# Three groups of 512 columns for branch A's projection, with branch B's values and gate moved into the keys' product

## The chip, the core and the metric

The kernel runs on one NeuronCore of one Trainium2 chip. The metric is the device time of one execution, in microseconds. The kernel before takes 1475.5 us (median of 3 runs, 1475.44 to 1475.64). The profile of an execution tells what each engine does: PE is the matrix engine (PEld are its weight loads), DVE the vector engine, ACT the scalar engine, POOL the general engine, SP the engine that only issues transfers.

## The reference

The input `x` has 2048 rows of 512. Two attentions over it are mixed by a gate.

```
g = sigmoid((x * gate_w).sum(-1))
# A: 32 heads of 16; each row attends to rows i, i-2, ..., i-14
q, k, v = x @ A_wqkv                      # 512 x 1536
a = softmax(q.k[i - 2w] * scale) . v[i - 2w]  @ A_wo
# B: 32 heads of 16 queries, all with the same keys and values
q = x @ B_wq ; k = x @ B_wk ; v = x @ B_wv    # k, v: 2048 x 16
b = softmax(q.k * scale) . v  @ B_wo          # over all 2048 rows
out = g * a + (1 - g) * b
```

## The kernel before

**Exactness.** Products of the projections run in a reduced format. So each operand is split in a high part and a low part (`split`, L82), and each product is made of three: high by high, high by low, low by high (`three`, L179). The depth of 512 is cut into four pieces `c`, so a projection of one bank is 12 steps. Each step is two matmuls, one on the upper and one on the lower 64 rows of the matrix engine; they run beside each other and write two halves of a pair of banks, which are added later.

**The start (0 to about 26 us).** `x` is loaded transposed in 16 blocks (`xraw`), and split into `xh` and `xl`. The keys' product (`keys`, L182) multiplies the unsplit `x` with a 128-column matrix made of the 512 x 16 key weights repeated: in each half of 64 columns there are the keys twice over interleaved, the keys once more, and once more again. The last 16 rows of each half are then overwritten by a constant in `post` (the scale in `mk[:, 0]` and the bias in `mk[:, 2]`): they are the rows through which a query's maximum is subtracted.

**The stream of lumps (about 26 to 268 us).** A list `lumps` holds 14 products for B's queries (`("q", m)`) and then 64 for branch A (`("a", gg, j)`): for each of four groups `gg` of 384 columns, 16 blocks `j` of 128 rows. In the first group 18 columns more ride along: 16 of B's values and 2 of the gate, which go to `vst` and `gate`. After each A lump, ACT copies the two half banks out (`a_post`, L251 and L252, and L254 and L255 for the values and the gate), POOL adds them (L261), and every second lump SP stores both to `ad` in device memory (L268). The weights of the next group are loaded by POOL's queue and split by ACT and POOL (`load_wa`, `split_wa`) while the current group runs, one piece every second lump. They lie in two buffers, each for a whole group.

**The maxima.** Branch B needs for each query the largest score before it can take exponentials. A unit is four heads by 512 queries; there are 32 units and 64 half fills for each, 2048 in all. A fill is a matmul into a spare bank and a reduction on DVE. `stream` (L732) puts fills between the lumps' steps, when the planner's own clock says that a bank is free: `clk["pe"]`, `clk["act"]` and `clk["dve"]` are moved on by fixed durations (`T_R` and so on, L46), and nothing is measured. Two forms exist: plain ones (`fill_pair` L352, `fill_one` L361), and after the first lumps of A a form through half sums and half differences (`fill_diff` L424, `fill_sum` L437): a pair of matmuls, two absolute values on ACT (L432), then two more matmuls, each with one DVE instruction (L442). One such round does four half fills.

**The attention of B (about 266 to 1461 us).** 512 steps `s`, 16 for each unit. A step has two exponentials of 128 x 1024 on ACT (L489), four pairs of half-array matmuls around them (`exp_pair` L482) and the weighted sum (`weighted` L494). Between them the planner puts fills of later units: one pair a step, and a single where `singles` (L890) finds that pairs alone will not be enough. Twelve of the 16 output blocks are made between units (`out_phase`), the last four in `spread`, which begins when the fills are all done and takes up to four products a step. If the fills of a unit are late, `pause` (L904) makes them with nothing beside. Branch A's own arithmetic is a list of pieces on POOL (`work`, L987), which starts when the first group is stored.

Of the kernel before, what the change touches and what calls it, by code (L numbers as in the profile page):

```python
# [33 lines left out]
GC = P // AC  # L34
GN = GC * AN
VN = DH + 2
# [6 lines left out]
LEAD, M2S, M1S, E1S, PER_ROW = 3.0, 0.5, 0.3, 0.2, 20  # L43

# [5 lines left out]
def gated_mix_kernel(ctx, tc, xt, wa, wk, wq, wo_a, wo_b, out):  # L50
# [53 lines left out]
    GO = [0, GN + VN, 2 * GN + VN, 3 * GN + VN]  # L104


    raw = []
    for pool, tag, n in ((wp, "aext", 5), (p1, "wah", 3), (p1, "wah", 3), (p1, "wal", 3), (p1, "wal", 2)):
        rest = pool.tile([P, n, 512], F32, name="xraw", tag=tag, bufs=2)
        raw += [rest[:, k, :] for k in range(n)]  # L110
# [17 lines left out]
    def load_wa(gg, c):  # L128
        n = GN + (0 if gg else VN)
        waraw[gg, c] = p1.tile([P, GN + VN], F32, name="waraw", bufs=2)  # L130
        nc.gpsimd.dma_start(waraw[gg, c][:, :n], wa[c * P:(c + 1) * P, GO[gg]:GO[gg] + n])

    def split_wa(gg, c):
        nonlocal pool
        n = GN + (0 if gg else VN)
        if c == 0:
            wah[gg] = p1.tile([P, C, GN + VN], F32R, name="wah", bufs=2)
            wal[gg] = p1.tile([P, C, GN + VN], F32R, name="wal", bufs=2)
        split(wah[gg][:, c, :n], wal[gg][:, c, :n], waraw.pop((gg, c))[:, :n], nc.gpsimd)
        pool = max(pool, clk["pe"] * 1e3) + 1100  # L140

    def ahead_wa(gg, k):
# [3 lines left out]
        if 2 < k <= 2 * C + 1 and k % 2:  # L146
            split_wa(gg, (k - 3) // 2)
# [34 lines left out]
    def keys(t):  # L182
# [49 lines left out]
    def a_project(gg, j):  # L232
        n = GN + (0 if gg else VN)
        t, r = j // 4, slice(j % 4 * P, (j % 4 + 1) * P)
        return three(lambda c: xh[t][c // 2][:, c % 2, r], lambda c: xl[:, t, c, r], lambda c: wah[gg][:, c, :n], lambda c: wal[gg][:, c, :n])

    def a_post(gg, j, x):

        nonlocal pool
        (bank, key), n = front[x], GN + (0 if gg else VN)  # L240
        settle("add", 1)
        if j % 2 == 0:
            settle("store", 1)
            stage["t"] = p1.tile([P, GC, 2, AN], F32, name="stage", bufs=2)
        st = stage["t"]
        if gg == 0 and j < 3:
            two = wp.tile([P, GN + VN], F32, name="two", tag="aext", bufs=2)
        else:
            two = (p2 if j % 3 else pm)[0].tile([P, GN + VN], F32, name="two", tag=("two", "raw", "own")[j % 3], bufs=1)
# [1024 lines left out]
```

## Time and profile before

| | |
|---|---|
| time, median of 3 runs | 1475.5 us |
| the profiled execution | 1475.43 us, of which the span of instructions is 1473.6 us |
| busy: PE, ACT, DVE, POOL | 99%, 86%, 81%, 70% of the span |
| A's lumps, first and last matmul | 76.0 us, 267.9 us |
| first and last start of an exponential (L489) | 266.5 us, 1460.1 us |

A busy share on PE is not a share of what it could do: its matmuls overlap, and their ends are modelled. So the prediction reads the distance from one start to the next. In a row of groups the numbers are: line, engine, operation, output and input, shapes, count, then busy time and mean duration in nanoseconds, then the idle time before and what ended it. In a row of waits they are the total, the number of times and the longest.

### The profile page before, as it was taken

Reading aid. Unit: us, or ns where it says so; the run is one execution under the profiler, and the core shown is the slowest. Engines: PE = TensorE matmul, PEld = TensorE weight load, DVE = VectorE, ACT = ScalarE, POOL = GpSimd, SP = SyncE. Lnnn points to the kernel's source line nnn. Section 1 sums busy time; section 2 is a strip of 40 time slices with the busy share of each in tenths; the row PEclk is TensorE's granted clock in tenths of the full one; section 3 lists DMA queues with packets and bytes.
Section 4 is the critical chain, followed back from the end, with each engine's and each line's share of the span. In section 5 each row is a group of like instructions: output and inputs, shape, how many; then the busy total and the mean of one; then the engine's idle time right before and its main releaser. Section 6 shows DMA issues by size and latency. Waiting matters only on the chain.

```text
span 1473.6 us, 29548 instructions
## 1 busy us (share of the span) xinstructions
PE 1461.7 (99%) x10996; PEld 708.0 (48%) x10996; DVE 1193.9 (81%) x1855; ACT 1274.5 (86%) x1646; POOL 1032.6 (70%) x1828
## 2 busy tenths in 40 slices
PE   9999999999999999999999999999999999999998
PEld 5999889533333333333333376333333364333333
DVE  6976667789888888888898878899888878889712
ACT  5468988899999999999999978999999988999986
POOL 7876988887888979888889898888888330111220
PEclk9999999999999999999999999999999999999999
DMA  6754323121220211202112121120120000000110
GB/s 224 209 151 136 93 88 120 34 85 42 66 80 7 85 60 42 71 12 71 45 38 77 36 64 67 42 71 26 57 71 12 12 27 16 13 1 2 29 31 30
DMA packets 54080, 89.86 MB, mean 61 GB/s; under 512 B 18800, under 2 KB 35232, under 8 KB 49712
## 3 DMA queue, kind: packets, MB, share of 16 engines
q1 hardware_dynamic: 46928, 48.99, 11.4%
q0 software_dynamic: 6432, 37.94, 7.8%
q8 instruction: 86, 1.41, 0.4%
q10 hardware_dynamic: 576, 1.05, 0.2%
q14 instruction: 58, 0.48, 0.1%
HBM read 60.07 MB, written 27.35 MB: 59 GB/s over the span
## 4 chain that ended last, share of the span: by engine, by line
PE 91%; ACT 3%; POOL 3%; issue 1%; DVE 1%; DMA 1%; DVEq 0%; POOLq 0%; ACTq 0%
PE po L497 35%; PE pe L487 23%; PE pm L330 8%; PE ps L330 7%; PE pe L1098 7%; PE pe L783 4%; PE pm L422 2%; PE ps L422 1%; PE pm L851 1%; ACT dd L432 1%; PE po L422 1%; POOL qlo L222 1%; POOL qraw L215 1%; PE pe L185 1%; DMA xraw<-xt 1%
## 5 line engine op out<-in xcount | busy, mean ns | idle before, releaser
L489 ACT ACTIVATE pexp<-pe 128x1024 f32<-128x1024 f32 x1022 | 989.5, 1022 | 93.0 <-PE pe L487 90.8
L357 DVE TENSOR_REDUCE mx<-pm 128x2 f32<-128x1024 f32 x495 | 605.8, 1224 | 117.6 <-PE pm L330 113.8
L497 PE MATMUL po<-pexp,vst 128*32 128x512 f32 x4096 | 545.7, 605 | 0.0
L487 PE MATMUL pe<-qst,kst 64*128 64x512 f32 x1916 | 434.5, 447 | 0.4 <-ACT pexp L489 0.3
L487 PEld LDWEIGHTS pe<-qst,kst 64*128 64x128 f32 x1916 | 179.7, 183 | 473.7 <-ACT pexp L489 467.8
L368 DVE TENSOR_REDUCE mx<-ps 128x1 f32<-128x512 f32 x481 | 327.1, 680 | 3.7 <-PE ps L330 3.7
L330 PE MATMUL pm<-kst,qst 62*128 62x512 f32 x945 | 192.0, 396 | 0.3 <-DVE mx L357 0.3
L561 POOL TENSOR_TENSOR pr<-aext 128x256 f32<-128x256 f32 x256 | 182.5, 738 | 2.2 <-DMA aext<-ad 1.9
L330 PE MATMUL ps<-kst,qst 62*128 62x512 f32 x455 | 180.0, 396 | 0.2 <-DVE mx L442 0.2
L621 POOL TENSOR_TENSOR oa<-oa,av 128x256 f32<-128x256 f32 x224 | 164.1, 732 | 15.1
L497 PEld LDWEIGHTS po<-pexp,vst 128*32 128x32 f32 x4096 | 80.8, 108 | 178.2 <-issue 169.1
L618 POOL TENSOR_TENSOR av<-aext,lg 128x256 f32<-128x256 f32 x224 | 139.3, 622 | 12.7
L1098 PE MATMUL pe<-wah,xh 64*128 64x384 f32 (+1 forms) x504 | 109.8, 338 | 0.4 <-ACT gate L255 0.4
L1098 PE MATMUL pe<-wal,xh 64*128 64x384 f32 (+1 forms) x504 | 110.1, 337 | 0.0
L1098 PE MATMUL pe<-wah,xl 64*128 64x384 f32 (+1 forms) x504 | 109.9, 337 | 0.0
L432 ACT ACTIVATE dd<-pm 128x512 f32<-128x512 f32 x164 | 91.0, 608 | 17.8 <-PE pm L422 11.3
L442 DVE CUSTOM_DVE_ANT_0 dd<-ps,dd 128x512 f32<-128x512 f32 x82 | 56.7, 692 | 55.1 <-PE ps L422 28.9
L330 PEld LDWEIGHTS pm<-kst,qst 62*128 62x128 f32 x945 | 92.0, 187 | 2.8 <-DVE mx L357 1.0
L330 PEld LDWEIGHTS ps<-kst,qst 62*128 62x128 f32 x455 | 85.0, 187 | 5.5 <-DVE mx L368 1.7
L567 POOL TENSOR_TENSOR tr<-pr 128x512 f32<-128x512 f32 x64 | 81.7, 1277 | 4.1
L567 POOL TENSOR_TENSOR tr<-tr 128x256 f32<-128x256 f32 (+1 forms) x128 | 72.4, 566 | 8.3
L524 POOL TENSOR_TENSOR rl<-rl,gate_t 128x16 f32<-128x16 f32 x31 | 6.8, 220 | 100.4 <-DVE rl L518 99.9
(215 smaller groups left out, 1896.2 us busy)
## 6 DMA issues: line engine op xcount, KB each, us to landing
aext<-ad POOLq DMA_DIRECT2D x32, 1056.0 KB, 5.5
ad<-stage SPq DMA_DIRECT2D x32, 384.0 KB
qst<-qd SPq DMA_DIRECT2D x60, 128.0 KB
xraw<-xt SPq DMA_DIRECT2D x16, 256.0 KB
qd<-qhi SPq DMA_DIRECT2D x16, 256.0 KB
qd<-qlo SPq DMA_DIRECT2D x16, 256.0 KB
qst<-qd SPq DMA_DIRECT2D x60, 64.0 KB
qst<-ml SPq DMA_DIRECT2D x216, 2.0 KB
```

Source lines behind the costliest of these rows:

```text
L330: nc.tensor.matmul(dst, qst[home(v)[0]][b:b + 62, pr, t * P:(t + 1) * P], kst[b:b + 62, kc * 512:(kc + 1) * 512], start=True, stop=True)
L357: nc.vector.tensor_reduce(m[:, :, pr, t, kc], dst, AX.X, ALU.max)
L368: nc.vector.tensor_reduce(m[:, odd, pr, t, kc:kc + 1], dst, AX.X, ALU.max)
L432: nc.scalar.activation(dd[0][:, odd], m2[:, odd, :], AF.Abs)
L487: nc.tensor.matmul(bank[:, odd, :], kst[b:b + 64, kt * P:(kt + 1) * P], qst[home(u)[0]][b:b + 64, pr, :], start=True, stop=True)
L489: nc.scalar.activation(e, bank, AF.Exp, scale=SCALE)
L497: nc.tensor.matmul(po[32 * i:32 * i + 32, :], vst[:, kt, :], pexp[s, i // 2][:, i % 2, :], start=(kt == 0), stop=(kt == NJ - 1))
L561: nc.gpsimd.tensor_mul(pr[:, k], q, e[:, o:o + NH, AC:2 * AC])
L567: nc.gpsimd.tensor_add(nx, cur[:, :, 0:n], cur[:, :, n:2 * n])
L618: nc.gpsimd.tensor_mul(av, e[:, o:o + NH, 2 * AC:].rearrange("p j (h d) -> p j h d", d=DH), lg[:, w].unsqueeze(3).to_broadcast([P, NH, AG, ...
L621: nc.gpsimd.tensor_add(ao, ao, av)
L1098: nc.tensor.matmul(front[2 if x == last else x % 2][0][:, b, :n], l[h], r[h], start=(i == 0), stop=(i == 3 * C - 1))
```

## The change

Branch A's 1536 columns are laid out group by head pair (`wa` is now in the order of `ad`), and are projected in 3 groups of 512 columns: 48 lumps instead of 64, each matmul 512 columns wide. A group boundary now falls inside a head pair, so a store of two lumps is made of pieces (`a_pieces`): whole head pairs, one transfer for each of the two lumps, and one or two part pairs. The values and the gate leave the first group; their weights take the last 16 columns of each half of the keys' matrix, which were overwritten anyway. A DVE transpose of each keys' bank is kept (`turned_k`), and 16 tasks of two small ACT copies bring them to `vst` and `gate`. The gate's exponential comes after query product 12 rather than at the end of the first group. The split weights lie in six single buffers for each part instead of two whole groups: pieces 2 and 3 of the next group are split during the last lump of the current one. Some of the planner's durations change.

```diff
-GC = P // AC
-GN = GC * AN
-VN = DH + 2
+GG = 3
+GN = NAG * AN // GG
+WB = 6
...
     def load_wa(gg, c):
-        n = GN + (0 if gg else VN)
-        waraw[gg, c] = p1.tile([P, GN + VN], F32, name="waraw", bufs=2)
-        nc.gpsimd.dma_start(waraw[gg, c][:, :n], wa[c * P:(c + 1) * P, GO[gg]:GO[gg] + n])
+        waraw[gg, c] = p1.tile([P, GN], F32, name="waraw", bufs=2)
+        nc.gpsimd.dma_start(waraw[gg, c], wa[c * P:(c + 1) * P, gg * GN:(gg + 1) * GN])
     def split_wa(gg, c):
...
-        if c == 0:
-            wah[gg] = p1.tile([P, C, GN + VN], F32R, name="wah", bufs=2)
-            wal[gg] = p1.tile([P, C, GN + VN], F32R, name="wal", bufs=2)
-        split(wah[gg][:, c, :n], wal[gg][:, c, :n], waraw.pop((gg, c))[:, :n], nc.gpsimd)
-        pool = max(pool, clk["pe"] * 1e3) + 1100
+        wah[gg, c] = p1.tile([P, GN], F32R, name="wah", bufs=WB)
+        wal[gg, c] = p1.tile([P, GN], F32R, name="wal", bufs=WB)
+        split(wah[gg, c], wal[gg, c], waraw.pop((gg, c)), nc.gpsimd)
+        after("act", clk["pe"], 0.62)
+        pool = max(pool, clk["pe"] * 1e3) + 1300
...
-        if 2 < k <= 2 * C + 1 and k % 2:
+        if 2 < k <= (2 * C if gg == 0 else 2 * (WB - C)) + 1 and k % 2:
             split_wa(gg, (k - 3) // 2)
...
             nc.vector.scalar_tensor_tensor(ks, pk, mk[:, 1:2], ks.bitcast(F32), op0=ALU.mult, op1=ALU.add)
+            nc.vector.transpose(turned_k[:, t, :], pk)
+    def values_of(t, q):
+        v = turned_k[32:64, t].rearrange("p (j b z) -> p j b z", b=4, z=32)[:, :, q, DH:2 * DH]
+        nc.scalar.activation(vst[32 * q:32 * q + 32, 4 * t:4 * t + 4, 0:DH], v, AF.Copy)
+        g = turned_k[96:128, t].rearrange("p (j b z) -> p j b z", b=4, z=32)[:, :, q, DH]
+        nc.scalar.activation(gate[32 * q:32 * q + 32, 1, 4 * t:4 * t + 4], g, AF.Copy)
+        after("act", clk["pe"], 0.45)
...
+    def a_store(st, gg, j, col, w, g, many, n):
+        src = st[:, :, col:col + w].rearrange("p j (g n) -> p g j n", g=many)
+        dst = ad[g:g + many, HALO:, :].rearrange("g (p j) n -> p g j n", j=NJ)[:, :, j - 1:j + 1, n:n + w // many]
+        if many > 1:
+            for x in range(2):
+                nc.sync.dma_start(dst[:, :, x], src[:, :, x])
+        else:
+            nc.sync.dma_start(dst[:, 0], src[:, 0])
...
-        nc.scalar.activation(own, bank[:, 0, :GN].rearrange("p (g n) -> p g n", g=GC), AF.Copy)
-        nc.scalar.activation(two[:, :n], bank[:, 1, :n], AF.Copy)
-        if gg == 0:
-            nc.scalar.activation(vst[:, j, 0:DH], bank[:, 0, GN:GN + DH], AF.Copy)
-            nc.scalar.activation(gate[:, 1, j:j + 1], bank[:, 0, GN + DH:GN + DH + 1], AF.Copy)
-        at = after("act", clk["pe"] + T_LAT, 0.8 if gg else 1.2)
+        nc.scalar.activation(own, bank[:, 0, :], AF.Copy)
+        nc.scalar.activation(two, bank[:, 1, :], AF.Copy)
+        at = after("act", clk["pe"] + T_LAT, 1.05)
...
-            nc.gpsimd.tensor_add(own, own, two[:, :GN].rearrange("p (g n) -> p g n", g=GC))
-            if gg == 0:
-                nc.gpsimd.tensor_add(vst[:, j, 0:DH], vst[:, j, 0:DH], two[:, GN:GN + DH])
-                nc.gpsimd.tensor_add(gate[:, 1, j:j + 1], gate[:, 1, j:j + 1], two[:, GN + DH:GN + DH + 1])
-            pool = max(pool, 1e3 * at) + (1000 if gg else 1450)
+            nc.gpsimd.tensor_add(own, own, two)
+            pool = max(pool, 1e3 * at) + 1280
+            def store():
+                for piece in a_pieces(gg):
+                    a_store(st, gg, j, *piece)
...
+    for k in range(16):
+        tasks.append((31.0 + 1.5 * k, values_of, divmod(k, 4)))
...
-                yield lambda: order[i][0] // GC < ready_gg
+                yield lambda: (AN * (order[i][0] + 1) - 1) // GN < ready_gg
...
-        return T_R if n == 512 else 0.18
+        return T_R
...
+        if lump[0] == "a" and lump[2] == NJ - 1 and lump[1] + 1 < GG and i in (4, 7) and WB - C < 4:
+            c = WB - C + (i == 7)
+            if c < C:
+                split_wa(lump[1] + 1, c)
...
+            if m == 12:
+                gates()
...
     def whole(gg):
         nonlocal ready_gg
-        if gg == 0:
-            gates()
         ready_gg += 1
...
+    wide = np.repeat(bk, 2, axis=1)
-        "wk": np.tile(np.concatenate([np.repeat(bk, 2, axis=1), bk, bk], axis=1), (1, 2)).reshape(C, P, P).transpose(1, 0, 2),
+        "wk": np.concatenate([wide, bk, bv, wide, bk, np.repeat(gw, DH, axis=1)], axis=1).reshape(C, P, P).transpose(1, 0, 2),
```

More of the change, by code (lines that the diff above doesn't have):

```diff
@@ L103, in gated_mix_kernel @@
     waraw, wah, wal = {}, {}, {}
[L104 to L110, printed above, removed]
+    first = wp.tile([P, 4, 512], F32, name="xraw", tag="aext", bufs=2)
+    raw = [first[:, k, :] for k in range(4)]
+    raw += [p1.tile([P, 512], F32, name="xraw", tag=tag, bufs=WB) for tag in ("wah", "wal") for _ in range(6)]
     xraw = {(t, c): raw[C * t + c] for t in range(NQB) for c in range(C)}
@@ L1074, in gated_mix_kernel @@
     lumps += [("q", m) for m in range(2, 4 * NQB)]
-    lumps += [("a", gg, j) for gg in range(C) for j in range(NJ)]
+    lumps += [("a", gg, j) for gg in range(GG) for j in range(NJ)]
     ready_gg, items = 0, {}
```

38 lines of the change are left out of this document (23 added, 15 removed).

## The prediction, made before the result was known

> **What bounds the kernel now.** I read the page first, then the stretches, then the order of time inside each stretch that the change touches.
>
> ```profile
> span 1473.6 us, 29548 instructions
> PE 1461.7 (99%) x10996; PEld 708.0 (48%) x10996; DVE 1193.9 (81%) x1855; ACT 1274.5 (86%) x1646; POOL 1032.6 (70%) x1828
> PE 91%; ACT 3%; POOL 3%; issue 1%; DVE 1%; DMA 1%; DVEq 0%; POOLq 0%; ACTq 0%
> ```
>
> The chain of work that ended last is PE's to 91%. So what counts is PE's work and the few places where PE waits. The stretches (times from the span's start; busy us of PE, PEld, DVE, ACT, POOL, with the number of instructions; then clock, DMA share, GB/s):
>
> ```profile
> 0.00:26.00 26.00, 24.45 (x72) 14.19 (x72) 14.21 (x27) 13.16 (x23) 18.99 (x25) 1.00 0.79 264
> 26.00:76.00 50.00, 49.23 (x416) 44.13 (x417) 48.05 (x61) 25.13 (x38) 45.19 (x39) 1.00 0.69 192
> 101.00:268.00 167.00, 165.87 (x1673) 151.77 (x1672) 111.54 (x345) 144.15 (x336) 137.71 (x223) 1.00 0.35 109
> 268.00:1392.00 1124.00, 1121.62 (x8053) 443.53 (x8051) 985.82 (x1361) 1017.53 (x1149) 795.10 (x1480) 1.00 0.14 44
> 1392.00:1473.00 81.00, 75.97 (x560) 32.11 (x558) 14.42 (x33) 61.84 (x66) 17.87 (x32) 0.99 0.12 30
> ```
>
> B's queries (26 to 76) have DVE and POOL full beside PE. In A's lumps with the half-sum fills (101 to 268) ACT is busy 144.15 of 167 us, the nearest to PE. From 268 to 1392 everything waits for steps of exponentials with fills between them; after 1392 there are no fills, only the last output blocks. The profiled execution took 1475.43 us, 1.8 us of them outside the span, 0.1 us under the median of 1475.5. My sum is made against 1475.4.
>
> **The lumps' matmuls.** Three excerpts of the order of time, for 512, 402 and 384 columns; the first and last start of an even run:
>
> ```profile
> 57.18 0.41 PE L1098 MATMUL pe<-xh,wqh 64*128 64x512 f32 x2
> 58.34 0.41 PE L1098 MATMUL pe<-xl,wqh 64*128 64x512 f32 x2
> ...
> 100.75 0.42 PE L1098 MATMUL pe<-wal,xh 64*128 64x402 f32 x2
> 101.86 0.41 PE L1098 MATMUL pe<-wal,xh 64*128 64x402 f32 x2
> ...
> 164.27 0.34 PE L1098 MATMUL pe<-wah,xl 64*128 64x384 f32 x2
> 164.98 0.34 PE L1098 MATMUL pe<-wah,xh 64*128 64x384 f32 x2
> ```
>
> They are 5, 6 and 4 steps apart, so a step takes 0.232, 0.185 and 0.1775 us. Before: 16 x 12 x 0.185 + 48 x 12 x 0.1775 = 35.5 + 102.2 = 137.7 us. After: 48 x 12 x 0.232 = 133.6 us. **Term 1: -4.1 us.** It is small because a step's time goes nearly with its columns: (0.232 - 0.1775) / 128 is 0.43 ns a column, which leaves 0.01 us a step that is saved by having fewer of them; the other half of the gain is the 18 columns of values and gate. The keys' product carries them free: its columns were computed before too.
>
> The Trainium skill, "TensorE: Matmul & The Clock Gate", section Back-to-back issue gap, gives columns / 2.4 + 2.5 ns for a warm matmul and so speaks against wide steps even more. By it the sum is 126.2 before and 124.3 after, a term of -1.9 and a total 2.2 us higher. Every step above is longer than this, 0.232 against 0.216 for 512, so I keep the rows.
>
> **What moves from ACT, POOL and DVE.** Groups of the lumps' stretches and of the start, and one line of the waits:
>
> ```profile
> L432 ACT ACTIVATE dd<-pm 128x512 f32<-128x512 f32 x164 | 91.0, 608 | 17.8 <-PE pm L422 11.3 <-DVE mx L442 5.9
> L252 ACT ACTIVATE two<-pe 128x384 f32<-128x384 f32 (+1 forms) x56 | 27.9, 499 | 0.0
> L251 ACT ACTIVATE stage<-pe 128x384 f32<-128x384 f32 x56 | 27.5, 492 | 5.2 <-PE pe L1098 3.0 <-POOL wal L84 0.8 <-PE po L422 0.4
> L442 DVE CUSTOM_DVE_ANT_0 dd<-ps,dd 128x512 f32<-128x512 f32 x82 | 56.7, 692 | 55.1 <-PE ps L422 28.9 <-ACT dd L432 23.2 <-ACT stage L251 1.4
> PEld pm L422 <- ACT dd L432: 11.3, 39, 0.7
> L83 ACT ACTIVATE wah<-waraw 128x384 fp32r<-128x384 f32 x11 | 5.9, 538 | 0.1
> L84 POOL TENSOR_TENSOR wal<-waraw,wah 128x402 fp32r<-128x402 f32 x4 | 3.9, 981 | 0.0
> L222 POOL TENSOR_TENSOR qlo<-qraw,qhi 128x512 fp32r<-128x512 f32 x14 | 18.1, 1290 | 5.4 <-ACT qhi L221 5.4
> L511 DVE STREAM_TRANSPOSE tt<-po 128x512 f32<-128x512 f32 x31 | 22.1, 714 | 1.1 <-PE po L497 0.5
> L287 ACT ACTIVATE gate_t<-gate 32x16 f32<-32x16 f32 x16 | 3.6, 228 | 0.4
> ```
>
> A copy of 512 columns is taken at the 608 ns of L432 (same shape). ACT's copies out: 64 x (499 + 492) = 63.4 us before, 48 x 2 x 608 = 58.4 us after.
>
> **Fewer maxima fit among the lumps.** The planner starts a round of four half fills when its own clocks say that ACT's absolute values are done. I walked these clocks by hand (L424 to L444 and L734 to L769). Undisturbed, a round lets 6 steps of 0.18 pass, or 5 steps of 0.23; a round into which a copy-out falls lets 8 or 7 pass. A lump of 12 steps is then 8 and two thirds of 6 before: 1.67 rounds, and 7 and 5 after: 2.0 rounds. Measured were 82 rounds (L442) in 56 lumps (L251), 1.46, which is 0.88 of the walk, as other ACT work disturbs it. After: 0.88 x 2.0 = 1.75 in the 40 lumps that are left after the same eight first ones: 70 rounds. So 12 rounds or 48 half fills fewer, less about 5 that the longer first eight lumps take in addition. A round is four matmuls in pairs, 2 x 0.232 us of PE. **Term 2: -5.6 us here**, paid back in term 6. Bounds: none lost (2.05 a lump) to 20 (1.55 a lump, if ACT's clock, now charged for the splits too, disturbs more rounds).
>
> **PE's waits among the lumps.** PE waited 11.3 us for the absolute values (the wait row). They come where ACT takes longer than planned: a copy-out is planned at 0.80 and takes 0.99 less overlap, a split of `wah` is not planned and takes 0.54. After, the copy-out is planned at 1.05 against 1.2 less overlap, and the split at 0.62. **Term 3: -4 us**; bounds 0 and -11.3. I take the lower third, since the two absolute values stay under-planned.
>
> **The queries' stretch gets slower.** The chain there, in order of time:
>
> ```profile
> 28.53 1.19 DVE mx L368 x2
> ...
> 60.25 0.89 POOL wal L84
> 61.14 1.26 POOL qlo L222
> ...
> 82.72 0.46 PE pe L1098 x2
> ```
>
> POOL's pieces run one behind the other. Four splits of the first group grow from 981 to 1290 ns: +1.2 us, which PE pays at 82.72, where the first of A's lumps waits for ACT behind the last query's parts. Four transposes of 714 ns come to DVE; three fall into the start, where it is busy 14.21 of 26 us, the fourth stands before the fills at 28.53: +0.7 us. The 32 small copies (228 ns each, 7.3 us in all) fit: ACT is busy 25.13 of 50 us there. If its gaps were not where they fall, two copies, 0.4 us, could delay each of eight queries, 3 us. **Term 4: +1.9 us**, bounds 0 and +5.
>
> **The weights at the two group boundaries.** Pieces 2 and 3 are split after steps 4 and 7 of the last lump and needed at steps 6 and 9 of the next, 14 steps later: with 1.75 rounds in a lump, (12 x 0.232 + 1.75 x 0.464) / 12 = 0.30 us a step, 4.2 us. In that time ACT must do 0.61 after what is queued, and POOL 1.29 each after its queue, which the planner lets run up to 2.5 us ahead plus one piece: 2.5 + 0.7 + 2 x 1.29 = 5.8, less the 0.9 us between the two. At the first boundary branch A's arithmetic has not begun, and POOL is free. Behind the waiting matmul PE's whole queue stands. **Term 5: +1.5 us**, at the second boundary; bounds 0 and +6.
>
> **Stores.** One transfer of 512 packets becomes three or four with 1536 in all.
>
> ```profile
> DMA  2000000000000499990000000000004999600000
> L268 SPq DMA_DIRECT2D ad<-stage x32: 359/366/396, 85.4 to 270.5; - x32
> 1152.44 0.73 POOL L621 TENSOR_TENSOR oa<-oa,av 128x256 f32<-128x256 f32 x1
> L672 PE MATMUL pe<-ident,oa x32: 213/222/274, 1187.0 to 1211.2; 64*128 64x64 f32 x32
> ```
>
> The first line cuts 160 to 172 us in 40; there are two stores in it. One holds the DMA engines for four slices of 0.3 us, 1.2 us. Three times the packets at the same time each would be 3.6 us, out of 7.3 us for two lumps (24 steps of 0.30). SP issues 4 x 0.37 us rather than 0.37, with nothing urgent behind it but queries' maxima for units far ahead. The buffer is used again three lumps after its last copy, 10.9 us, less the copies and POOL's add (1.2 + 1.29): 8.4 us. Cost 0; without that cover see the rivals. Branch A's arithmetic starts when the first group is stored, 16 x 12 x (0.232 - 0.185) = 9 us later; it ended at 1153 and its last results are first used at 1187, so that is hidden too.
>
> **The end.** What was not filled early must be filled late:
>
> ```profile
> 1372.16 1.07 PE L497 MATMUL po<-pexp,vst 128*32 128x512 f32 x8
> 1380.75 1.07 PE L497 MATMUL po<-pexp,vst 128*32 128x512 f32 x8
> 1382.64 1.07 PE L497 MATMUL po<-pexp,vst 128*32 128x512 f32 x8
> 1390.70 1.07 PE L497 MATMUL po<-pexp,vst 128*32 128x512 f32 x8
> 1392.03 0.88 PE L851 MATMUL pm<-woh,turned 64*128 64x512 f32 x6
> 1422.19 0.63 PE L851 MATMUL pm<-wol,own 64*128 64x512 f32 x4
> 1424.30 0.39 PE L851 MATMUL pm<-wol,own 64*128 64x512 f32 x2
> L357 DVE TENSOR_REDUCE mx<-pm 128x2 f32<-128x1024 f32 x468 | 572.9, 1224 | 111.8 <-PE pm L330 108.1 <-PE ps L330 0.2
> ```
>
> Four steps with a pair and a single take 8.59 us, 2.15 each; four with the pair alone 8.06, 2.02. Singles ran almost to the end: about five steps at 1382 to 1391 had room for one. So of 43 more half fills 5 are cheap (0.13 us each), and 38 need 13 further steps of three. The last blocks, which began at 1392.03 and ran three products in 2.11 us steps, then have 20 steps instead of 33 for their 84 products (ten may follow): four a step, 20 x 0.232 = +4.6 us. The fills of the last unit are also due by step 488, some four steps too early; the rest goes in a pause at 1.22 us a pair (L357) with little beside, +2.4 us. **Term 6: +7 us**; bounds 0 (no rounds lost) and +23 (19 pairs all in pauses).
>
> **Sum.** -4.1 - 5.6 - 4 + 1.9 + 1.5 + 7 = -3.3, so 1472.1 us, called **1472 us**. About 3 us, 0.2%, is what a measurement here can tell from no change.
>
> **The rivals.**
> *The fills keep up* (22%). If the rounds stay at 82, nothing is moved, terms 2 and 6 go, and shorter lumps are kept whole: -4.1 - 4 + 1.9, without the stall: 1469; with the longer waits gone too, 1464. For it: two full rounds a lump in the walk. Against it: 0.88 of them ran.
> *The end overflows* (24%). If 60 half fills or more are missing, the last unit's maxima are not ready, and each further pair is a pause of 1.22 us: 10 pairs more, +12 us, about 1483. It decides from some 50 missing half fills on. For it: DVE is busy 986 of the 1124 us from 268 to 1392 already. Against it: the output blocks' own rounds lie between.
> *The weights come late* (10%). Both boundaries at the full bound: +6 rather than +1.5, with the queries at +5: 1479.
> *The stores hold the staging buffers* (4%). If a short packet takes twice as long, a store takes 8 us and more, and every third lump waits about 1 us, some 20 us: 1490. The low load (0.35 of the engines) speaks against it.
>
> **Chances.** The forecast itself has 40%, with its own range of 1468 to 1476, half of it under 1472.5. Faster by over 0.2%: half of 40 and the 22, 42%. Within: the other half and a part of the late weights, 25%. Slower: 33%. The range over the cases is 1463 to 1484.
>
> **What would show it.** 48 lumps at 0.232 us a step; A's last lump ending some 8 us earlier, at 260; 70 rounds (L442 with `dd` 140) instead of 82; the queries' stretch ending 2 us later; the last blocks' products starting nearer to the last exponential. Wrong would be: as many rounds as before, PE waiting for `wal` or `wah` by microseconds, waits of ACT for `stage` stores, or pauses before step 496.

## The result and the profile after

The kernel after takes 1477.97 us (median of 20 runs, 1477.59 to 1480.71), the kernel before beside it 1475.42 us (20 runs, 1475.21 to 1476.48). The ratio is 1.0019 with a 95% interval of 1.0012 to 1.0026: the change makes the kernel slower by about 0.2%. The prediction said 1472 and faster.

The page of the profile after, its span, its engines and the chain of work that ended last:

```profile
span 1475.9 us, 28719 instructions
...
PE 1462.1 (99%) x10612; PEld 681.4 (46%) x10612; DVE 1210.2 (82%) x1851; ACT 1269.2 (86%) x1592; POOL 1023.9 (69%) x1772
...
PE 87%; DVE 1%; ACT 1%; SPq 1%; issue 0%; DMA 0%; DVEq 0%; ACTq 0%; POOL 0%
```

PE does less (10612 matmuls instead of 10996), but holds only 87% of the chain instead of 91%, and SP's queue has appeared in it with 1%. The stretches, columns as in the prediction:

```profile
101.00:268.00 167.00, 165.98 (x1360) 129.59 (x1360) 111.15 (x318) 139.40 (x272) 130.78 (x184) 1.00 0.40 108
268.00:1392.00 1124.00, 1122.58 (x8065) 444.06 (x8057) 987.55 (x1365) 1016.56 (x1146) 798.78 (x1485) 1.00 0.14 43
1392.00:1475.00 83.00, 75.13 (x529) 33.20 (x521) 26.86 (x44) 53.87 (x57) 15.54 (x28) 0.96 0.10 27
```

In the last one DVE is busy for 26.86 us instead of 14.42: there are fills now. And the clock, 0.99 before, is 0.96 on the mean. Where the time goes is seen best from the start of a step's first weighted matmul (L497 before, L518 after; 8 a step, read from the order of time):

| | before | after | difference |
|---|---|---|---|
| step 0 starts at | 269.1 | 260.6 | -8.5 |
| step 0 to 480 | 1124.0 | 1122.4 | -1.6 |
| 480 to 484 | 9.4 | 8.5 | -0.9 |
| 484 to 488 | 9.6 | 14.2 | +4.6 |
| 488 to 492 | 8.7 | 11.6 | +2.9 |
| 492 to 496 | 8.7 | 11.4 | +2.7 |
| 496 to 511 | 31.6 | 35.3 | +3.7 |
| 511 to the end of the span | 12.4 | 11.8 | -0.6 |

At step 480 the kernel after is 10.1 us ahead. In the last 32 steps it loses 12.4. The lead is that of one trace: seven kernels below are edits that have the same lumps, and their traces reach step 480 8.5 to 10.4 us ahead, but for `a_kt0`, which spends more time before it. The order of time of PE at the end:

```profile
1397.12 0.40 PE L351 MATMUL pm<-kst,qst 62*128 62x512 f32 x2
1397.35 0.40 PE L508 MATMUL pe<-qst,kst 64*128 64x512 f32 x2
1397.60 0.39 PE L351 MATMUL ps<-kst,qst 62*128 62x512 f32 x1
1397.91 1.06 PE L518 MATMUL po<-pexp,vst 128*32 128x512 f32 x8
1398.91 0.51 PE L351 MATMUL pe<-kst,qst 62*128 62x512 f32 x2
1399.24 0.40 PE L351 MATMUL pm<-kst,qst 62*128 62x512 f32 x2
1399.48 0.40 PE L351 MATMUL pe<-kst,qst 62*128 62x512 f32 x2
1400.80 0.51 PE L351 MATMUL pe<-kst,qst 62*128 62x512 f32 x2 [0.93 <-DVE mx L378]
1401.93 0.50 PE L351 MATMUL pm<-kst,qst 62*128 62x512 f32 x2 [0.62 <-DVE mx L378]
1404.19 1.22 PE L508 MATMUL pe<-qst,kst 64*128 64x512 f32 x4 [1.76 <-DVE mx L378]
1405.21 0.62 PE L351 MATMUL ps<-kst,qst 62*128 62x512 f32 x1
1405.77 1.93 PE L518 MATMUL po<-pexp,vst 128*32 128x512 f32 x8
...
1410.98 1.10 PE L872 MATMUL pm<-woh,turned 64*128 64x512 f32 x8
...
1413.58 1.09 PE L872 MATMUL pm<-wol,turned 64*128 64x512 f32 x8
...
1424.46 0.69 PE L508 MATMUL pe<-qst,kst 64*128 64x512 f32 x2 [0.59 <-DMA qst<-ml]
```

Until 1398.9 the steps still have a pair and a single (L351). Then a pause: five pairs with nothing beside, the last two, and the step behind them, held up by DVE's reductions (L378). The first step behind it is odd: its eight weighted matmuls take 1.93 us, where the same eight took 1.06 at 1397.91. The stretches from the pause on say why; the clock is the third number from the end:

```profile
1398.91:1404.19 5.28, 1.97 (x14) 0.85 (x10) 5.14 (x6) 0.41 (x1) 0.00 (x0) 0.92 0.01 2
1404.19:1410.64 6.45, 6.45 (x27) 2.05 (x27) 3.46 (x7) 3.88 (x4) 0.34 (x2) 0.54 0.00 0
1410.64:1424.46 13.82, 13.24 (x106) 6.28 (x103) 1.90 (x5) 10.24 (x10) 6.33 (x12) 1.00 0.20 41
```

PE is busy for 1.97 of the 5.28 us of the pause. Before the pause ends its clock is halved, and it stays so nearly to the end of the next two steps. These two steps have 13 matmuls each (four for the exponentials, one fill, eight weighted) and take 6.45 us together; the same 26 take 4.00 us at full clock in `a_busy`, below. So the low clock costs 2.45 us. Behind that the products of the last blocks (L872) come four a step, 2.59 us from one step to the next. In the kernel before they come three a step, 2.36 us, and later two, 2.12 us. So the 12.4 us are, about: 5.3 us of pause and 2.45 of low clock (together the 7.5 between steps 484 and 492, within 0.3), then 6.4 us of crowded steps, the 0.59 us wait at 1424.46 among them, less the 1.5 us in the first and last row.

### The profile page after: what moved, and what is told of

The parts are those of the page before. It is cut to its first block, busy times and chain, and to the rows that moved or that the text cites. A ratio compares the mean times of both kernels' runs of the same rounds, so it can differ in the third digit from the quotient of the medians.

```text
span 1475.9 us, 28719 instructions
## 1 busy us (share of the span) xinstructions
PE 1462.1 (99%) x10612; PEld 681.4 (46%) x10612; DVE 1210.2 (82%) x1851; ACT 1269.2 (86%) x1592; POOL 1023.9 (69%) x1772
## 3 DMA queue, kind: packets, MB, share of 16 engines
q1 hardware_dynamic: 68176, 49.00, 11.7%
q10 hardware_dynamic: 576, 1.05, 0.2%
## 4 chain that ended last, share of the span: by engine, by line
PE 87%; DVE 1%; ACT 1%; SPq 1%; issue 0%; DMA 0%; DVEq 0%; ACTq 0%; POOL 0%
PE po L518 34%; PE pe L508 23%; PE pm L351 8%; PE ps L351 7%; PE pe L1124 5%; PE pe L804 4%; PE pm L443 2%; PE ps L443 1%; PE po L443 1%; PE pm L872 1%; SPq L728 0%; DVE mx L378 0%; PE pe L693 0%; ACT pexp L453 0%; DMA td<-raw 0%
## 5 line engine op out<-in xcount | busy, mean ns | idle before, releaser
L378 DVE TENSOR_REDUCE mx<-pm 128x2 f32<-128x1024 f32 x500 | 611.8, 1224 | 117.7 <-PE pm L351 114.8
L518 PE MATMUL po<-pexp,vst 128*32 128x512 f32 x4096 | 546.8, 606 | 0.1
L389 DVE TENSOR_REDUCE mx<-ps 128x1 f32<-128x512 f32 x494 | 336.1, 680 | 4.5 <-PE ps L351 4.5
L351 PE MATMUL pm<-kst,qst 62*128 62x512 f32 x942 | 192.2, 396 | 0.9 <-DVE mx L378 0.9
L351 PE MATMUL ps<-kst,qst 62*128 62x512 f32 x459 | 181.9, 396 | 0.4 <-DVE mx L463 0.2
L518 PEld LDWEIGHTS po<-pexp,vst 128*32 128x32 f32 x4096 | 80.6, 108 | 180.1 <-issue 171.6
L453 ACT ACTIVATE dd<-pm 128x512 f32<-128x512 f32 x150 | 85.0, 609 | 24.3 <-PE pm L443 21.2
L1124 PE MATMUL pe<-wal,xh 64*128 64x512 f32 x376 | 94.4, 392 | 0.2 <-POOL wal L84 0.2
L1124 PE MATMUL pe<-wah,xh 64*128 64x512 f32 x376 | 93.8, 392 | 0.1
L351 PEld LDWEIGHTS pm<-kst,qst 62*128 62x128 f32 x942 | 92.0, 187 | 3.7 <-DVE mx L378 1.6
L1124 PE MATMUL pe<-wah,xl 64*128 64x512 f32 x376 | 92.9, 392 | 0.0
L463 DVE CUSTOM_DVE_ANT_0 dd<-ps,dd 128x512 f32<-128x512 f32 x75 | 51.9, 692 | 48.3 <-PE ps L443 39.9
L351 PEld LDWEIGHTS ps<-kst,qst 62*128 62x128 f32 x459 | 85.8, 187 | 6.6 <-DVE mx L389 2.4
L281 POOL TENSOR_TENSOR stage<-stage,two 128x512 f32<-128x512 f32 x48 | 62.5, 1302 | 23.1 <-ACT two L275 22.6
```

The costliest lines, as they stand in the source:

```text
L351: nc.tensor.matmul(dst, qst[home(v)[0]][b:b + 62, pr, t * P:(t + 1) * P], kst[b:b + 62, kc * 512:(kc + 1) * 512], start=True, stop=True)
L378: nc.vector.tensor_reduce(m[:, :, pr, t, kc], dst, AX.X, ALU.max)
L389: nc.vector.tensor_reduce(m[:, odd, pr, t, kc:kc + 1], dst, AX.X, ALU.max)
L453: nc.scalar.activation(dd[0][:, odd], m2[:, odd, :], AF.Abs)
L518: nc.tensor.matmul(po[32 * i:32 * i + 32, :], vst[:, kt, :], pexp[s, i // 2][:, i % 2, :], start=(kt == 0), stop=(kt == NJ - 1))
L1124: nc.tensor.matmul(front[2 if x == last else x % 2][0][:, b, :], l[h], r[h], start=(i == 0), stop=(i == 3 * C - 1))
```

## The experiments

Every time below is given with the ratio to the kernel before, run on the same chip beside it, and its 95% interval. Kernels whose names begin with `a_` are edits of the kernel after, with `b_` of the kernel before.

### Is it the fills that are late?

`a_drop32` leaves out half of the last unit's fills, so its maxima are those of half the keys.

```diff
     slots += [(v, pr, t, kc) for v in range(2, NU) for pr in range(2) for t in range(4) for kc in range(4)]
+    slots = [x for x in slots if x[0] < NU - 1 or x[3] < 2]
...
-                left[x] = NF // NU
+                left[x] = NF // NU // (1 + (x == NU - 1))
```

> The changed kernel without the last unit's half fills over the third and fourth block of keys: 32 of its 64 are left out, so its maxima are taken over half of the keys. Theory (the end is short of fills, because the planner made 28 fewer before the attention began): the pause and the crowded last blocks go, 13 us less, about 1465. Rival (the time is lost at the end by something else that the change moved, such as branch A's later start or the transfers): only the fills' own time goes, 32 at 0.13 us at most, about 1474.

Measured: 1466.91 us, 0.9937 (0.9923 to 0.9952). From step 480 to the end it takes 81.3 us, almost the 80.5 of the kernel before. No stretch has a low clock:

```profile
1396.00:1412.00 16.00, 16.00 (x126) 6.99 (x124) 2.06 (x4) 13.00 (x14) 3.67 (x6) 1.00 0.19 39
```

`b_act105` does the reverse: in the kernel before, the planner's charge for a copy-out is raised, so that fewer rounds are started among the lumps and more fills are left for later.

```diff
-        at = after("act", clk["pe"] + T_LAT, 0.8 if gg else 1.2)
+        at = after("act", clk["pe"] + T_LAT, 1.05 if gg else 1.2)
```

> The kernel before with the same number raised: the copy-out of the groups after the first is charged at 1.05 us instead of 0.80, nothing else. Theory: it makes some 10 rounds fewer, 40 half fills are missing, the attention starts about 4 us earlier and 14 us or more are lost at the end: 1485. Rival (the end is not sensitive to missing fills): 1472 to 1476.

Measured: 1481.49 us, 1.0035 (1.0022 to 1.0048). This is 3.5 us less than the theory said. Step 0 starts at 259.5 us, 9.6 earlier than before, and step 480 to the end takes 95.9 us instead of 80.5. The same pause, the same half clock, in a kernel without the change:

```profile
1393.00:1407.20 14.20, 11.11 (x69) 4.13 (x68) 12.63 (x13) 7.85 (x9) 0.00 (x0) 0.87 0.01 2
1407.20:1409.00 1.80, 1.80 (x9) 0.20 (x8) 0.69 (x1) 1.26 (x2) 0.00 (x0) 0.50 0.00 0
```

So the loss is the late fills', and not that of the wider matmuls, the stores or the values.

`a_kt0` gives the late fills room: singles are allowed in the first step of every unit from the eighth on, not only of the last eight.

```diff
-                if not later_rows and (kt or not s or u >= NU - 8) and singles(s):
+                if not later_rows and (kt or not s or u >= 8) and singles(s):
```

> The changed kernel with single fills also allowed in the first step of each unit from unit 8 on (before only from unit 24 on): 16 more places. Theory: the fills are done at about step 485 with no pause, 8 to 10 us less, about 1469. Rival (the first step of a unit has no room, as DVE transposes the output there): each place costs what it saves, 1476 to 1478.

Measured: 1475.61 us, 0.9996 (0.9986 to 1.0005), a miss. The end is nearly mended (82.1 us from step 480), but steps 0 to 480 take 1130.0 us instead of 1122.4. Set beside the kernel after step by step, each of the 16 new places costs 0.23 to 0.25 us, 3.8 in all, so the first steps have little room, as the rival said. Another 2.2 us go between steps 271 and 272, where output blocks are made; why, and where the last 1.6 go, was not followed further.

### What are the shorter lumps worth?

`a_act080` and `a_act085` lower the charge for a copy-out in the kernel after, so that more rounds are started; `a_act060` goes further. `b_act085`, `b_act090` and `b_act060` are the controls in the kernel before (the last with 0.9 in place of 1.2 in the first group).

```diff
-        at = after("act", clk["pe"] + T_LAT, 1.05)
+        at = after("act", clk["pe"] + T_LAT, 0.8)
```

> The changed kernel with one number of the planner set back: a copy-out of a lump is charged to its ACT clock at 0.80 us, not 1.05. Theory: rounds among the lumps come back to 82 (150 instructions of L463 with dd become 164), the attention starts some 3 us later than in the changed kernel, the end is that of the kernel before; 1475.4 less the 5 us by which the lumps end earlier than before, about 1470. Rival (the rounds are held down by ACT itself and not by its planned charge): rounds that are planned wait on the chip, the lumps get 7 us longer, 1478 or more.

> The kernel after with the charge of a copy-out at 0.85 instead of 1.05. The planner's account has 1628 half fills left at step 0 and 5 at step 480 (1616 and 2 with 0.80; 1644 and 39 with 1.05). Theory (what is left at step 480 sets the loss at the end, and 5 fit into the steps there): step 0 at about 264, 2 to 3 us earlier than with 0.80, the end as with 0.80 but for 1 us, in all about 1470.5. Rival (the end is lost as soon as more than before is left): 1474 or more.

> The kernel after with the charge of a copy-out at 0.60 instead of 1.05. The planner's account has 1592 half fills left at step 0 (1616 with 0.80). Theory (a half fill costs 0.12 us of PE among the lumps and 0.13 as a single later, so moving one saves nothing once the end has room, and waits for absolute values grow): step 0 some 4 us later than with 0.80, the end unchanged, 1472 to 1474 in all, no gain over 0.80. Rival (each half fill taken out of the attention is worth what it cost at the end, 0.4 us): 24 x 0.4 = 10 us less, 1463.

> The same charge, 0.85 instead of 0.80, in the kernel before (later groups only): 1628 half fills left at step 0 and 5 at step 480, as in the version of the kernel after with 0.85. Theory: step 0 some 2 us earlier, 1 us of it given back at the end, 1474 to 1475; the two kernels with the same account then differ by the shorter lumps, 3 to 4 us. Rival (what is gained by the charge 0.85 is worth the same to the kernel before, and no advantage of the shorter lumps remains): 1471.

> The kernel before with the charge at 0.90: the account has 1636 left at step 0 and 18 at step 480, with no pause. Between the 2 of the kernel before and the 39 of the kernel after, whose stretch from step 480 to the end takes 13 us more. Theory A (each half fill that is late costs the same, 13 / 37 = 0.35 us): the stretch is 5 to 6 us longer than before. Theory B (they are cheap, 0.13 us, until they cannot be made in steps and pauses begin): 2 us longer.

> A control on the kernel before: the charge of a copy-out at 0.60 instead of 0.80 (0.90 instead of 1.20 in the first group), about as far below its measured 0.99 as 0.80 is below the 1.20 of the kernel after. The account has 1572 half fills left at step 0 instead of 1616. Theory (the gain of the version with charge 0.80 is the change's, shorter lumps, not that of an optimistic charge): 1474 to 1477, no gain over before. Rival (an optimistic charge gains by itself, whatever the lumps): 1472 or less.

`a_384` keeps four groups of 384 columns in the kernel after, with the rest of the change: the values and the gate in the keys' product, the six single buffers. Its charge is that of `a_act080`, so the two differ by the width.

```diff
-GG = 3
+GG = 4
...
-        at = after("act", clk["pe"] + T_LAT, 1.05)
+        at = after("act", clk["pe"] + T_LAT, 0.8)
...
-        return T_R
+        return T_R if lump[0] == "q" else 0.18
```

> Half of the change: the values and the gate ride in the keys' product, the weights lie in six single buffers, stores are two transfers for two lumps, but branch A is projected in 4 groups of 384 columns as before, with the charge of a copy-out at 0.80. The planner's own account has 1620 half fills left at step 0, against 1616 before, so the end is not disturbed. Theory (a step goes with its columns, so that the 18 columns gone are worth 16 x 12 x 0.0075 = 1.4 us and the width itself the rest): about 1474.5, and the version with 512 columns and the same charge stays 2 us below it. Rival (the width is worth nothing, the whole gain is the move of the values and the gate): about 1472.3, the same as the version with 512 columns and the charge 0.80.

The table counts half fills between the first lump of A and step 0. "Rest" is this stretch less the lumps' matmuls (137.7 us before, 133.6 with three groups, 136.3 for `a_384`) and less 0.116 us for each half fill: what is left is mostly waiting.

| | half fills | stretch | rest | step 0 to 480 | 480 to end | time | ratio |
|---|---|---|---|---|---|---|---|
| before | 354 | 192.9 | 14.1 | 1124.0 | 80.5 | 1475.4 | 1 |
| after | 327 | 183.9 | 12.4 | 1122.4 | 92.9 | 1477.97 | 1.0019 (1.0012 to 1.0026) |
| `a_act085` | 343 | 187.6 | 14.2 | 1125.9 | 80.8 | 1472.97 | 0.9980 (0.9971 to 0.9989) |
| `a_act080` | 355 | 190.1 | 15.3 | 1123.8 | 79.8 | 1472.32 | 0.9975 (0.9965 to 0.9984) |
| `a_act060` | 379 | 198.6 | 21.0 | 1121.2 | 79.8 | 1477.53 | 1.0014 (1.0005 to 1.0024) |
| `a_384` | 351 | 193.0 | 16.0 | 1123.9 | 79.8 | 1475.03 | 0.9997 (0.9988 to 1.0006) |
| `b_act105` | 314 | 183.2 | 9.1 | 1125.0 | 95.9 | 1481.49 | 1.0035 (1.0022 to 1.0048) |
| `b_act090` | 334 | 190.0 | 13.6 | 1125.6 | 83.4 | 1477.07 | 1.0011 (1.0002 to 1.0020) |
| `b_act085` | 342 | 192.1 | 14.7 | 1125.3 | 81.6 | 1476.64 | 1.0007 (0.9999 to 1.0016) |
| `b_act060` | 398 | 206.4 | 22.5 | 1123.2 | 80.4 | 1489.23 | 1.0093 (1.0077 to 1.0108) |

The theories put `a_384` and `b_act090` about right (1474.5 us; 2 us more at the end). `a_act080` and `a_act085` came out 2.3 and 2.5 us above theirs, and `b_act085` 1.6 above. `a_act060` and `b_act060` missed by 3.5 and 12 us: with so many rounds the rest grows by 6 and 8 us.

A caution on the columns of single traces: the eight traces with the lumps of the kernel after (its own, `a_drop32`, `a_kt0` and the five of the next section) have stretches of 183.5 to 185.9 us, 185.2 in the middle, and rests of 12.0 to 14.4. So a difference of 2 us between two of these rows says nothing by itself; the times are medians and say more.

Four things follow.

First, the gain of the shorter lumps is real. With as many half fills as before (`a_act080`) it is 0.25%, and no charge that was tried gives the kernel before anything (`b_act085`, `b_act060`).

Second, it comes from the width: `a_384`, which has all but the width, is where the kernel before is.

Third, the rest goes with the number of half fills: 9.1, 13.6, 14.7 us for 314, 334, 342 in the kernel before, 12.4 and 14.2 for 327 and 343 in the kernel after. No effect of the lumps' width on it stands out of the scatter. The total of the waits of PE's weight loads for ACT's absolute values is a poor measure of it. It nearly doubled in `a_act080`, while the rest there is 1.2 us above before. The waits of the kernel after, then of `a_act080` (total, times, longest; the row of before, 11.3 us, stands in the prediction):

```profile
PEld pm L443 <- ACT dd L453: 11.7, 36, 0.8
```

```profile
PEld pm L443 <- ACT dd L453: 21.2, 69, 1.5
```

A single long wait does count. In the eight traces with the same lumps the total of this row goes from 11.0 us (`a_sp`, longest 0.4) to 13.6 (`a_kt0`, longest 2.6), and the rest goes with it, 12.0 to 14.4.

Fourth, steps 0 to 480 take 1121 to 1126 us whether 1572 or 1656 half fills are left for them. How many are over at step 480, by the planner's account: 2 of the 1616 left in the kernel before, 5 of 1628 (both kernels at 0.85), 18 of 1636 (`b_act090`), 39 of the 1644 in the kernel after. So 1614, 1623, 1618 and 1605 were made in these steps. The kernel before had room for about a dozen more, and not for 20; why the kernel after made the fewest is not shown. A half fill that is moved from the lumps saves about 0.2 us there (190.1 less 185.2, over 28, is 0.18), and beyond that room it falls into the last 32 steps. The loss there is not proportional. With 18 over (`b_act090`) it is 2.9 us, 0.16 each; with 39 it is 12.4. This is nearer to the second theory of `b_act090`, cheap until pauses begin: its trace has no pause and no low clock there. `a_act060` shows the other side: 24 half fills that are kept among the lumps cost 8.5 us and save 2.6 later.

### What is the loss at the end made of?

`a_busy` gives PE something to do in the pause: the first three of four equal pairs of matmuls are overwritten.

```diff
-    def fill_pair(dst, key):
+    def fill_pair(dst, key, again=0):
         v, pr, t, kc = slots.pop(0)
         m = unit_tile(v)
+        for odd in [0, 1] * again:
+            max_mm(dst[:, odd, :], v, pr, t, kc, odd)
...
-            fill_pair({"e0": eb[0], "e1": eb[1], "m2": m2}[key], key)
+            fill_pair({"e0": eb[0], "e1": eb[1], "m2": m2}[key], key, 3)
```

> The kernel after, but a pair of fills that is made in a pause runs its two matmuls four times into the same bank before the reduction reads it (the first three are idle work, PE only). In the kernel after PE is busy 1.97 of the 5.28 us of the pause, and then the granted clock is 0.54 for 6.45 us (0.50 in the slices from 1404 to 1410). Theory (the clock falls because PE does too little in the pause): with 5 x 4 x 0.232 = 4.6 us of work in it the clock stays at 1.00 and the 26 matmuls behind the pause take 3.7 us (2.13 us for the 15 of a step with a pair and a single) instead of 6.45; the first reduction of the pause starts 0.7 later; in all 2 us less than after, about 1476. Rival (the low clock has another cause, the end of the program or the matmuls' form): the clock still falls, 1478.5 or more.

Measured: 1480.16 us, 1.0032 (1.0019 to 1.0044). The time is a miss, but the mechanism is shown. The clock stays whole in the pause and behind it, and the 26 matmuls of the next two steps take 4.00 us (the second line):

```profile
1402.84:1406.26 3.42, 2.62 (x24) 1.75 (x20) 3.42 (x4) 0.00 (x0) 0.00 (x0) 1.00 0.01 2
1406.51:1410.51 4.00, 4.00 (x26) 1.28 (x26) 2.96 (x6) 3.41 (x4) 0.00 (x0) 1.00 0.00 0
```

From step 488 to 492 it takes 9.9 us instead of 11.6. What it won is lost again at step 496, in the order of time of PE and in that of SP:

```profile
1425.85 0.73 PE L510 MATMUL pe<-qst,kst 64*128 64x512 f32 x2 [2.13 <-DMA qst<-ml]
...
1413.26 8.64 SPq L730 DMA_DIRECT2D oa<-td  x16
1422.01 2.60 SPq L498 DMA_DIRECT2D qst<-ml  x4
```

PE waits for the maxima of the last unit, and behind this wait its clock is halved after all:

```profile
1426.74:1430.15 3.41, 3.41 (x17) 1.23 (x13) 0.00 (x0) 1.99 (x2) 0.00 (x0) 0.50 0.16 25
```

So steps 492 to 496 take 14.6 us instead of 11.4. SP issues four of the maxima's transfers only behind 16 transfers that bring the turned rows of a last output block. In the kernel after it is the same, order of time of POOL and SP:

```profile
1410.86 0.25 POOL L481 TENSOR_TENSOR ml<-mt,mh 128x32 fp32r<-128x32 f32 x1
1411.46 2.26 POOL L496 DMA_DIRECT2D qst<-ml  x4 [0.34 <-POOL ml L481]
...
1413.12 7.43 SPq L728 DMA_DIRECT2D oa<-td  x16
1420.65 2.60 SPq L496 DMA_DIRECT2D qst<-ml  x4
```

The maxima are ready at 1411.1. POOL's half of the transfers goes out at once, SP's half more than nine microseconds later. The low clock had hidden this: PE came so late that it waited only 0.59 us.

`a_due3` lets the fills run into steps nearer to their unit, so that the pause shrinks.

```diff
-        steps = 16 * v - 6 - s
+        steps = 16 * v - 3 - s
```

> The kernel after, but the fills of a unit may be made up to 3 steps before it begins instead of 6, before a pause is called. The account then has pauses for 2.2 and 2.0 half fills instead of 9.2 and 1.0; the rest of the late fills goes into steps. Theory (of the 13 us lost from step 480 on, the pause and the low clock behind it are about 8): 5 to 6 us less than after, 1472 to 1473, with a granted clock of 1.00 throughout. Rival (the last unit's maxima are then late for step 496, since their transfers stand behind the 16 of the last output blocks on SP): the wait takes the pause's place, 1477 or more.

Measured: 1483.39 us, 1.0054 (1.0042 to 1.0067): the rival. At step 492 it is 6.8 us ahead of the kernel after, and then waits for 9.03 us. During that wait the clock is halved, from 1421.3 to 1431.6. Order of time of PE and SP:

```profile
1425.84 0.99 PE L508 MATMUL pe<-qst,kst 64*128 64x512 f32 x2 [9.03 <-DMA qst<-ml]
...
1414.50 7.43 SPq L728 DMA_DIRECT2D oa<-td  x16
1422.03 2.60 SPq L496 DMA_DIRECT2D qst<-ml  x4
```

`a_sp`, `a_due3sp` and `a_due4sp` move the 16 transfers: with 6, 3 and 4 steps in the line above, they start a block's turning 11 products later.

```diff
-                if i == 1 and j + 2 <= js[-1]:
+                if i == 3 * C and j + 2 <= js[-1]:
```

> The kernel after, with one line moved: the turning of the third and fourth of the last output blocks, and with it SP's 16 transfers, begins at product 12 of the block two ahead of it instead of product 1. In the kernel after the low parts of the last unit's maxima are ready at 1411.11; POOL issues its four transfers at 1411.46, SP its four only at 1420.65, behind those 16. Theory (that order costs the 0.59 us which PE waits at step 496, and no more as long as the pause and the low clock stand before it): 0.5 to 1 us less than after, 1477 to 1477.5. Rival (the order costs nothing, the blocks are then late): 1478 or more.

> Both edits: fills of a unit may be made up to 3 steps before it begins, and SP's 16 transfers come later. With the first alone PE waited 9.03 us at step 496 for the last unit's maxima, whose transfers SP issued at 1422.03 though they were ready at 1412.5. Theory (the place of the 16 transfers makes that wait): it falls to at most 2 us, and the pause and the low clock are gone too: 1473 to 1475, 8 to 10 us less than the first edit alone. Rival (the maxima are late by the fills themselves): the wait stays above 5 us, 1479 or more.

> As the one before, with 4 steps instead of 3: the account has a pause for 4.2 half fills and one for 2.0, and the last fills one step earlier. Theory: the pause costs 2 to 3 us more than with 3 steps, the wait for the maxima 1 to 2 us less: within 1.5 us of it, 1473 to 1475. Rival (the wait for the maxima decides): at least 2 us less than with 3 steps.

Measured: `a_sp` 1477.59 us, 1.0013 (1.0005 to 1.0022); `a_due3sp` 1472.45 us, 0.9980 (0.9971 to 0.9989); `a_due4sp` 1475.43 us, 0.9999 (0.9990 to 1.0008). In `a_due3sp` SP issues the maxima's transfers at once, step 496 waits for nothing, and the clock is whole where the pause was; order of time of SP, then the stretch:

```profile
1412.40 2.93 SPq L496 DMA_DIRECT2D qst<-ml  x4
1420.87 0.35 SPq L722 DMA_DIRECT2D td<-raw  x1
1422.91 7.42 SPq L728 DMA_DIRECT2D oa<-td  x16
```

```profile
1396.00:1412.00 16.00, 15.25 (x106) 5.23 (x106) 11.70 (x14) 13.65 (x15) 0.44 (x2) 1.00 0.01 1
```

The same edit is worth 0.4 us where the pause stands before it (`a_sp`; 0.9 by the ratios, and inside what the two vary) and 11 us where the pause is gone (`a_due3` to `a_due3sp`). `a_due4sp` missed: its shorter pause still halves the clock, by 1407.5, and it is 3 us slower than `a_due3sp`. By the mean clock, not each execution of it is hit: two of the eleven have a mean clock of 1.000 and take 1473.76 and 1473.87 us, the others 0.998 or 0.999 and 1474.58 to 1477.08.

```profile
1407.00:1407.50 0.50, 0.00 (x0) 0.00 (x0) 0.50 (x1) 0.00 (x1) 0.00 (x0) 0.91 0.00 0
1407.50:1408.00 0.50, 0.35 (x2) 0.29 (x2) 0.09 (x1) 0.00 (x0) 0.00 (x0) 0.50 0.00 0
```

Three versions beat both kernels: `a_act080` and `a_act085`, which leave few fills late, and `a_due3sp`, which lets them be late without a pause. Their times, 1472.32, 1472.97 and 1472.45 us, can't be told apart by their intervals. Both kinds of edit in one kernel were not run.

## Why the prediction was wrong

**Term 6, the end, was mis-sized, and it decided the sign.** It stood at +7 us; the last 32 steps lost 12.4. The mechanism was the one described: late fills, four products a step, a pause. The step that failed is the pause. I had the fills due four steps too early and charged 2.4 us, which is two pairs; but four steps of three are twelve half fills, six pairs. Five pairs it was, 5.3 us, and then the half clock, 2.45 us, which the working did not have at all. A pause before step 496 was among the working's own signs of being wrong. It came with only 27 half fills moved instead of 43, as the steps between made fewer than in the kernel before (1605 and 1614, by the planner's account); why is not shown.

The crowded steps came near (4.6 us predicted for four products a step, 6.4 measured with the small wait), but partly by luck. The working took 2.11 us for a step with three products. In the order of time of PE in the kernel before, a step with three (x6) takes 2.36 us, and one with two (x4) takes 2.12:

```profile
1397.80 1.07 PE L497 MATMUL po<-pexp,vst 128*32 128x512 f32 x8
1399.14 0.86 PE L851 MATMUL pm<-woh,turned 64*128 64x512 f32 x6
1400.16 1.06 PE L497 MATMUL po<-pexp,vst 128*32 128x512 f32 x8
...
1418.74 1.07 PE L497 MATMUL po<-pexp,vst 128*32 128x512 f32 x8
1420.08 0.62 PE L851 MATMUL pm<-woh,own 64*128 64x512 f32 x4
1420.86 1.06 PE L497 MATMUL po<-pexp,vst 128*32 128x512 f32 x8
```

So two products a step ran before for most of the end, and the kernel after pays for a third and a fourth.

**The rival "the end overflows" was the right one, but for its threshold.** It was to decide from 50 missing half fills on. By the account it decided at 28. With 20 missing (`b_act090`) there was no pause yet.

**Term 1 (-4.1) holds.** The first and the fourth step of a run in the last lump, in the order of time of the kernel after, give (258.43 - 257.73) / 3 = 0.233 us a step:

```profile
257.73 0.42 PE L1124 MATMUL pm<-wal,xh 64*128 64x512 f32 x2
...
258.43 0.41 PE L1124 MATMUL pm<-wal,xh 64*128 64x512 f32 x2
```

`a_act080`, with the half fills of before, is 2.8 us shorter in the lumps' stretch; 1.2 us more of rest takes the difference. The part that I put down to the 18 columns of values and gate is a third of the term by its own rows (16 x 12 x 0.0075 = 1.4 us), not half, and it does not show: `a_384` gained 0.3 us, inside its interval.

**Term 2 (-5.6, 12 rounds) was too large.** 7 rounds were lost, 82 to 75; with the other fills 27 half fills, 3.1 us at 0.116 each.

```profile
L453 ACT ACTIVATE dd<-pm 128x512 f32<-128x512 f32 x150 | 85.0, 609 | 24.3 <-PE pm L443 21.2 <-DVE mx L463 2.9
```

**Term 3 (-4, fewer waits) did not come as put.** The row on which it rested went from 11.3 to 11.7 us. The rest fell by 1.7 us in this trace, by 0.5 in the middle of the eight with the same lumps, and it falls as far in the kernel before with as few fills (13.6 us with 334, 9.1 with 314). So the total of the row was no price. The likely reason is that a weight load that waits 0.3 us lies beside the matmul of the other half, which runs for 0.4; this is argued and was not tested. Only a long wait is seen in the stretch, as the eight traces show.

**Term 4 (+1.9)** was +0.5 us: the first lump of A starts at 76.7 instead of 76.2. **Term 5 (+1.5)**: PE's weight loads waited 1.1 us for `wal`. Together the five terms gave -10.3 us, and -10.1 was measured at step 480. That they agree is luck: the terms all lie before step 0, where -8.5 was measured, and 1.6 us came between step 0 and step 480 unasked. Of the terms, the rounds and the waits were put too large, and the queries and the weights too, in the other direction.

**The stores** cost nothing that shows, as predicted: no row of after has ACT waiting for `ad`.

## What to carry to other kernels

Before you move work out of a stage, ask how much room the stages behind it have left, and read it from the first one that has to be done by a fixed time. Here a dozen items more cost about 1 us at the end (`b_act085`), and 28 more cost 12.4, twice what they saved. When a wait is removed and the time does not fall, look at what the engine waits for next and at the order of the queue that brings it: here the same moved line was worth less than 1 us or 11 us, according to what stood before it. The total of a row of many short waits of weight loads is not their price; compare the stretch itself.

## What was unexpected of the hardware

PE's granted clock fell to 0.50 in a pause in which it was never idle for longer than 1.76 us at a stretch. By the first two lines below (0.63 of a quarter of a microsecond, then 0.72) it fell at 1403.31 and was whole again at 1410.14, 6.83 us later. When it fell, the gap of 1.76 us had lasted only 0.9 us, as it began at 1402.43. So the length of that gap did not decide. In the 3.41 us before the fall PE was busy for 1.01 us, the third line (stretches of the kernel after; the clock is the third number from the end):

```profile
1403.25:1403.50 0.25, 0.00 (x0) 0.00 (x0) 0.25 (x1) 0.00 (x0) 0.00 (x0) 0.63 0.00 0
1410.00:1410.25 0.25, 0.25 (x8) 0.00 (x0) 0.25 (x2) 0.25 (x1) 0.02 (x1) 0.72 0.00 0
1399.90:1403.31 3.41, 1.01 (x4) 0.37 (x4) 3.41 (x4) 0.00 (x0) 0.00 (x0) 1.00 0.01 2
```

In `a_due4sp` PE was busy for 1.79 of the 3.41 us before the fall, and the fall came inside a single gap of 1.77 us, 1.5 us after its start. In the pause of `a_busy` it was busy for 2.62 of 3.42 us, with a gap of 1.05 us, and the clock stayed. The Trainium skill, "TensorE: Matmul & The Clock Gate", section Why this matters for your kernels, asks for no idle gaps of more than about 3 us. Here the gaps were shorter, so the measurement decides: shorter gaps with little work between them can be too much.

The traces give one more regularity. The low clock lasted 3.41 us in `a_sp` and behind the wait in `a_busy`, 6.83 in the kernel after and in `a_due4sp`, and 10.24 in `a_due3`: once, twice and three times the same length. The full clock between two falls of the kernel after lasted 64.85 us (1410.14 to 1474.99), 19 times 3.41. This looks as if the clock were set anew every 3.41 us by the work before, and it would explain why executions of one kernel differ: in `a_sp`, with the same pause as in the kernel after, the low clock lasted half as long. That is inferred from these lengths. No threshold follows: in `a_drop32` PE was busy for 1.58 of the 3.41 us from 1458.74 on, among the last products, and the clock stayed whole behind it.
